# A decode step of attention beside a squared-ReLU MLP on one core: wq loaded ahead of the first K unit, output sums kept as two plain halves

## The chip, the core and the metric

The kernel runs on one core of a Trainium2 chip. The metric is device time in microseconds (us), as the median of three timed runs. "Faster" or "slower" is meant against that median. All instruction times come from one profiled execution of the kernel. In the names below, PE is TensorE's matmuls and PEld its weight loads, DVE is VectorE, ACT is ScalarE, POOL is GpSimd, and SP is SyncE, which here does nothing but issue transfers.

## What is computed

Two tokens (B = 2) of width D = 576 pass one layer norm, and the result feeds two branches whose outputs are added to the input.

```python
xn  = layernorm(x)                                  # 2 x 576
q   = xn @ wq                                       # 32 heads of 128
k,v = last 2048 positions of the caches, 16 heads, each shared by 2 query heads
A   = softmax(q k^T / sqrt(128)) v @ wo             # wo: 4096 x 576
h   = relu(xn @ w1 + b1); h = h * h                 # 4608 wide
B   = h @ w2 + b2                                   # w2: 4608 x 576
out = x + A + B                                     # 2 x 576, bf16
```

Everything is bf16 in memory. The windows of K and V are 16.8 MB each, and the four weight matrices add 20.1 MB, so that about 53.6 MB must be read for an output of 2.3 KB.

## The kernel before

**Units.** K and V are cut into eight units each, four heads of one batch row at a time. A unit is one transfer of 2 MB into one of six slots of a pool (`kvpool`, tag `kv`), 16 KB in each of 128 partitions. wq, w1 and wo share one slot of another pool (`wbig`), in that order. All these loads are issued by SP, in program order (lines 130 to 136, 415, 421, 426 to 433 and 435 to 441). A load into a slot that is in use waits in SP's queue until the slot's last reader is done, and every load behind it waits too.

**Start.** The order of the first loads is K unit 0 (line 130), wq (131), K1, V0, K2, V1, K3. Meanwhile the layer norm of x and a set of small masks and identities are made. PE then transposes K0 (`transposes(0, g)`, line 410: eight groups of four transposes into PSUM, copied out by ACT and DVE in turn), and after that `q_block` (line 411, defined at 226) computes q with 36 matmuls of 512 columns, copies the rows out (238), transposes them and spreads them into `qz` (254). Then come the scores and the softmax of unit 0 (lines 413 and 414).

**Steady part.** `step(u)` (line 387) transposes K unit u, with the product of probabilities and V of unit u-2 between the groups, then scores and softmax. `mlp_h` (356) computes h from w1 when w1 has landed (line 434), and puts it, transposed, into `hT_sb`. The result of attention stands, transposed, in `ws` (351).

**Output sums.** The sum `x + b2 + A + B` is accumulated in one PSUM tile `out_ps`. `out_acc` (216) takes one block of 128 rows of wo or w2, that is 576 columns, as four matmuls of 144 columns, one on each of the four strips of 32 columns of the array (`tile_position=(0, 32 * i)`). The two batch rows stand 16 partitions apart (`BS = 16`, `MB = 17`), so a weight operand has 17 columns, 15 of them zeros that two POOL memsets (310, 312) write at the start. The order on PE, which the program fixes (`keep_in_program_order`), is: 32 blocks of wo (line 446), 18 blocks of `w2a` (448), then 9 of `w2b` and 9 of `w2c` (451). `w2c` arrives by three transfers of 6, 2 and 1 blocks (`W2P`, line 76), the last loads of the kernel. So each of the blocks 9, 15 and 17 waits for a landing of its own.

**Store.** ACT issues one store of `w2b`'s first bytes to the output when w2b has landed (line 455), then casts `out_ps` to bf16 (456), 113 partitions by 144 columns, and stores the result over the first one (457), as a pattern of 4 quarters by 2 rows by 144 elements, that is, eight pieces of 288 bytes.

Of the kernel before, what the change touches and what calls it, by code (L numbers as in the profile page):

```python
# [8 lines left out]
F32 = mybir.dt.float32  # L9
BF16 = mybir.dt.bfloat16  # L10
ACT = mybir.ActivationFunctionType
ALU = mybir.AluOpType
AX = mybir.AxisListType
# [3 lines left out]
def kernel(  # L17
# [14 lines left out]
    nc = tc.nc  # L32
    P = 128
    B, Sq, D = A_x.shape
    _, Hkv, Sk, Dh = A_k_cache.shape
# [25 lines left out]
    NG4 = 4  # L61
# [10 lines left out]
    WR = Hq * Dh // P  # L72
    WC = Dh // WR
    FR = L1 // P
    assert HW == 32 * FR and QH * 2 == NC and NC * WC == 32
    W2P = [(9, 15), (15, 17), (17, 18)]
    R9 = 9
    BS = 16
    MB = BS * (B - 1) + 1
    RM = 32 * (NG4 - 1) + MB  # L80
    OQ = D // 4
    BIG = 1e30

    const = ctx.enter_context(tc.tile_pool(name="const", bufs=1))
# [4 lines left out]
    work = ctx.enter_context(tc.tile_pool(name="work", bufs=2))  # L89
    keep = ctx.enter_context(tc.tile_pool(name="keep", bufs=2))  # L90
    psum = ctx.enter_context(tc.tile_pool(name="psum", bufs=1, space=bass.MemoryType.PSUM))

    def matmul(*a, **k):
        tc.keep_in_program_order(nc.tensor.matmul(*a, **k))  # L94
# [15 lines left out]
    def load_k(u):  # L110
        issue_kv(k_tiles, A_k_cache, u, "k")
# [4 lines left out]
    def issue_flat(w, name):  # L116
        n = w.shape[0] * w.shape[1] // P
        tl = wbig.tile([P, NH * L1], BF16, tag="wbig", name=name)
        nc.sync.dma_start(out=tl[:, 0:n], in_=w.rearrange("r n -> (r n)").rearrange("(p l) -> p l", p=P))
        return tl  # L120

    const.tile([P, 144], F32, name="pad_0")
    xb_sb = const.tile([B + 1, D], BF16, name="xb_sb")
    x_sb = xb_sb[0:B, :]
    nc.scalar.dma_start(out=x_sb, in_=x2d)
# [1 line left out]
    nc.vector.memset(eps_t[:], 1e-5)  # L127
    warm = const.tile([B, 2], F32, name="warm")
    nc.scalar.activation(out=warm[:, 0:1], in_=eps_t[:], func=ACT.Sqrt)
    load_k(0)  # L130
    wq_sb = issue_flat(A_wq, "wq")
    load_k(1)
    load_v(0)
    load_k(2)
# [15 lines left out]
    nc.vector.tensor_scalar(out=ident[:], in0=col_f, scalar1=row_f[:, 0:1], scalar2=None, op0=ALU.is_equal)  # L150
    ident_f = const.tile([P, P], F32, name="ident_f")
    nc.vector.tensor_scalar(out=ident_f[:], in0=col_f[:], scalar1=row_f[:, 0:1], scalar2=None, op0=ALU.is_equal)
    sel_b = const.tile([B + 1, MB], BF16, name="sel_b")
    nc.vector.memset(sel_b[:], 0.0)
    nc.vector.memset(sel_b[:, 0:MB:BS], 1.0)
    nc.vector.tensor_copy(out=sel_b[0:B, 0:MB:BS], in_=ident[0:B, 0:B])

    half_d = D // 2
    stats = const.tile([B, 2, 6], F32, name="stats")
# [50 lines left out]

    w2c_sb = w2pool.tile([P, (FR - R9) * D], BF16, name="w2c")

    out_ps = psum.tile([RM, OQ], F32, tag="out", name="out_ps")
    nc.vector.memset(out_ps[:], 0.0)

    def out_acc(lhsT, rhs, o, start=False, stop=False):
        for i in range(4):
            matmul(out_ps[32 * i:32 * i + MB, :], lhsT=lhsT, rhs=rhs[:, o * D + i * OQ:o * D + (i + 1) * OQ],
                   start=start, stop=stop, skip_group_check=True, tile_position=(0, 32 * i))

    qz = const.tile([P, NQ, B, 2, 3 * QZ], BF16, name="qz")
    nc.gpsimd.memset(qz[:], 0.0)
    q_ps = psum.tile([P, QW], F32, tag="o", name="q_ps")
    nc.vector.memset(q_ps[:], 0.0)

    def q_block():
        for t in range(NH):
            for g in range(NG4):
                o = t * LQ + g * QW
                matmul(q_ps[32 * g:32 * g + 2 * B, :], lhsT=xnT[:, t].rearrange("p x b -> p (x b)"),  # L230
                       rhs=wq_sb[:, o:o + QW], start=(t == 0), stop=(t == NH - 1), skip_group_check=True,
                       tile_position=(0, 32 * g))
        row_t = const.tile([RB, 4 * HW], BF16, tag="row", name="qrow")
        qrow = row_t[:, 0:2 * QW]
        nh = QH // 2
        for k in range(2):
            cp = nc.scalar.copy if k else nc.vector.tensor_copy
            cp(out=qrow[:, k * QW:(k + 1) * QW].rearrange("p (i a d) -> p i a d", a=2, d=Dh),  # L238
               in_=q_ps[0:RB, k * QW // 2:(k + 1) * QW // 2].rearrange("p (i d) -> p i d", d=Dh).unsqueeze(2)
               .to_broadcast([RB, nh, 2, Dh]))  # L240
        qrow_f = qrow.bitcast(F32)
        qT_ps = psum.tile([P, QH * P], F32, tag="sc", bufs=2, name="qT_ps")
        for i in range(QH):
            transpose(out=qT_ps[:, i * P:i * P + RB], in_=qrow_f[:, i * Dh:(i + 1) * Dh],
                      identity=ident_f[0:RB, 0:RB])
        qT_v = qT_ps[:].bitcast(BF16).rearrange("p (i g e x b c) -> p b x g c e i", g=NG4 // 2, e=2, x=32 // B, b=B, c=2)
        hd = Dh // 2
        for j2 in range(2):
            cp = nc.scalar.copy if j2 else nc.vector.tensor_copy
            pp = slice(hd * j2, hd * (j2 + 1))  # L250
            o = QZ + NC * j2
            for b in range(B):
                for half in range(2):
                    cp(out=qz[pp, half * NQ // 2:(half + 1) * NQ // 2, b, :, o:o + NC].rearrange(  # L254
                        "p g c (e i) -> p g c e i", e=2), in_=qT_v[pp, b, half])
# [50 lines left out]
        pT_tiles[u] = pT  # L306
        o1_tiles[u] = o1

    ws = const.tile([P, WR, MB], BF16, name="ws")
    nc.gpsimd.memset(ws[:], 0.0)  # L310
    hT_sb = const.tile([P, 2, FR, MB], BF16, name="hT_sb")
    nc.gpsimd.memset(hT_sb[:], 0.0)

    def pv(u, part, parts):
        n = NJJ // parts
# [10 lines left out]
    def pv_end(u):  # L326
        tq, b = divmod(u, B)
        o_ps = o_tiles.pop(u)
        o1 = o1_tiles.pop(u)
        for k in range(NS):  # L330
            kw = dict(out=o1[:, 0:Dh], in0=o_ps[:, k * Dh:(k + 1) * Dh])
            if k == 0:
                nc.vector.tensor_scalar(scalar1=in_s[:, 0:1], scalar2=None, op0=ALU.mult, **kw)
            else:
                nc.vector.scalar_tensor_tensor(scalar=in_s[:, k:k + 1], in1=o1[:, 0:Dh], op0=ALU.mult, op1=ALU.add,  # L335
                                               **kw)

        def fin():
            op = psum.tile([P, Dh + 1], F32, tag="op", name=f"op_ps_{u}")
            pp = slice(32 * tq, 32 * (tq + 1))  # L340
            matmul(op[pp, :], lhsT=of_h[:], rhs=o1[:], start=True, stop=True, skip_group_check=True,
                   tile_position=(0, 32 * tq))
            linv = work.tile([P, 1], F32, tag="linv", name=f"linv_{u}")
            nc.vector.reciprocal(out=linv[pp, :], in_=op[pp, Dh:Dh + 1])
            om_t = work.tile([P, Dh], F32, tag="om", name=f"om_{u}")
            om = om_t[pp, :].rearrange("p (q r) -> p q r", r=WR)
            nc.vector.scalar_tensor_tensor(out=om, in0=op[pp, 0:Dh].rearrange("p (q r) -> p q r", r=WR),
                                           scalar=linv[pp, 0:1], op0=ALU.mult, op1=ALU.mult,
                                           in1=own_c[pp, :].unsqueeze(2).to_broadcast([32, WC, WR]))
            with nc.allow_low_precision(reason="sums of one term and zeros"):  # L350
                nc.vector.tensor_reduce(out=ws[pp, :, BS * b], in_=om.rearrange("p q r -> p r q"), axis=AX.X,  # L351
                                        op=ALU.add)

        return fin

    def mlp_h(w1_sb):
# [20 lines left out]
        for a in range(2):  # L377
            hp = psum.tile([P, nr, RB + 4], BF16, tag="sc", bufs=2, name=f"hp_{a}")
            for r in range(nr):
                transpose(out=hp[:, r, 0:RB], in_=hrow[:, a * nr + r:4 * HW:FR], identity=ident[0:RB, 0:RB])  # L380
            for g in range(NG4):
                pp = slice(32 * g, 32 * (g + 1))
                cp = nc.scalar.copy if g % 2 else nc.vector.tensor_copy
                cp(out=hT_sb[pp, :, a * nr:(a + 1) * nr, 0:MB:BS].rearrange("p x r b -> p r x b"),
                   in_=hp[pp, :, 32 * g:32 * g + 2 * B].rearrange("p r (x b) -> p r x b", b=B))

    def step(u):
# [17 lines left out]
    def pv_all(u):  # L405
        pv(u, 0, 1)
        pv_end(u)()

    for g in range(NG):
        transposes(0, g)  # L410
    q_block()
    for t in range(NT):
        scores(0, t)
    softmax(0)
    load_v(2)
    b1_rows = B_b1.rearrange("(x n) -> x n", n=HW)
    for i0, i1 in ((0, 2), (2, 4), (4, 6), (6, 8)):
        nc.scalar.dma_start(out=b1_sb[i0:i1, :], in_=b1_rows[i0:i1, :])
    nc.scalar.dma_start(out=xb_sb[B:B + 1, :], in_=B_b2.rearrange("(o n) -> o n", o=1))
    step(1)  # L420
# [21 lines left out]
    step(NU - 1)  # L442
    pv_all(NU - 2)
    pv_all(NU - 1)
    for r in range(WR):
        out_acc(ws[:, r, :], wo_sb, r)
    for r in range(FR):
        out_acc(hT_sb[:, 0, r, :], w2a_sb, r)
    for r in range(FR):
        w, o = (w2b_sb, r) if r < R9 else (w2c_sb, r - R9)  # L450
        out_acc(hT_sb[:, 1, r, :], w, o, stop=(r == FR - 1))

    fin_sb = work.tile([RM, OQ], BF16, tag="fin", name="fin_sb")
    out_v = out2d.rearrange("b (q n) -> q b n", q=4)
    nc.scalar.dma_start(out=out_v, in_=w2b_sb[0:RM:BS, 0:OQ])
    nc.scalar.copy(out=fin_sb[:], in_=out_ps[:])  # L456
    nc.scalar.dma_start(out=out_v, in_=fin_sb[0:RM:BS, :])


# [28 lines left out]
```

## Time and profile before

| | us |
|---|---|
| timed runs | 134.02, 134.00, 133.95 (median 134.0) |
| profiled execution, first to last instruction (span) | 132.1 |
| median less span: what lies around the span | 1.9 |
| PE, DVE, ACT busy | 84.6, 63.2, 46.7 |
| HBM read over the span | 53.62 MB, 406 GB/s |
| last matmuls (w2c) begin, in the span | 127.90 |
| cast of the output, begin | 129.29 |
| store of the output issued | 129.60 |

The profiled execution has no time of its own beside its span, so 1.9 us is the distance from that span to the median of the three runs. The profile has a page of totals, a list of what ended each wait, a chain of work that ended last, a timeline, and tables by window, that is, busy times in stretches of time that one chooses. In tables by window, the columns are the stretch, its length, the busy time of each engine with its instructions in brackets, the clock that TensorE was granted (1.00 is full speed), the mean busy share of the 16 DMA engines, and GB/s. All times count from the first instruction.

### The profile page before, as it was taken

To read this page: it belongs to the slowest core of one execution; us is meant where nothing else is said; L and a number is where in the kernel's file an instruction comes from. 1 tells how busy PE (TensorE), PEld (TensorE's weight loads), DVE (VectorE), ACT (ScalarE), POOL (GpSimd) and SP (SyncE) were. 2 spreads that over 40 slices of the span, in tenths; PEclk is the share of its full clock that TensorE was granted. 3 is DMA by queue.
4 is the path that set the end of the run, shared out by engine and by line. 5 is a ranking of instruction groups with operands and counts; after the bars stand their busy time and mean duration, and the time that the engine had idled before them with its cause. 6 is when DMAs were issued, how large, how long until landed. Compare 5 with 4: busy or idle time off the path is not lost.

```text
span 132.1 us, 2285 instructions
## 1 busy us (share of the span) xinstructions
PE 84.6 (64%) x949; PEld 52.6 (40%) x949; DVE 63.2 (48%) x176; ACT 46.7 (35%) x67; POOL 4.9 (4%) x15
## 2 busy tenths in 40 slices
PE   0089319599589687697599787104819972739471
PEld 0069202286345353363455443002417640229360
DVE  7764400344557677396547687410075667550000
ACT  5725400339566085283256094200106632000000
POOL 5000000010010100100100100100000001000000
PEclk9999955959999999999779999855695999555955
DMA  4999899999999999999999999999999999899960
GB/s 160 397 437 526 369 388 442 422 432 432 429 432 422 442 417 427 437 432 437 432 427 414 437 488 402 445 424 405 427 427 442 468 435 458 376 408 418 418 255 1
DMA packets 3511, 53.76 MB, mean 407 GB/s; under 512 B 419, under 2 KB 558, under 8 KB 814
## 3 DMA queue, kind: packets, MB, share of 16 engines
q1 hardware_dynamic: 3456, 53.61, 95.2%
q8 instruction: 7, 0.11, 0.3%
q10 hardware_dynamic: 46, 0.02, 0.1%
q14 instruction: 2, 0.02, 0.0%
HBM read 53.62 MB, written 0.00 MB: 406 GB/s over the span
## 4 chain that ended last, share of the span: by engine, by line
DMA 78%; PE 15%; ACT 2%; SPq 1%; DVE 1%; issue 1%; ACTq 0%; DVEq 0%
DMA w<-in_B_w_dram 25%; DMA w2c<-in_B_w_dram 24%; DMA k<-in_A_k_cache_dram 16%; DMA wq<-in_A_wq_dram 13%; PE kT_ps L97 5%; PE h_ps L94 3%; PE q_ps L94 3%; PE sc_ps L94 2%; PE out_ps L94 1%; PE o_ps L94 1%; ACT kT L270 1%; DVE qrow L238 1%; SPq L106 0%; ACT qrow L238 0%; DVE qz L254 0%
## 5 line engine op out<-in xcount | busy, mean ns | idle before, releaser
L97 PE MATMUL kT_ps<-ident_f,k 128*128 128x128 f32 x256 | 41.4, 312 | 5.7 <-DMA k<-in_A_k_cache_dram 3.9
L97 PEld LDWEIGHTS kT_ps<-ident_f,k 128*128 128x128 f32 x256 | 32.9, 161 | 18.8 <-issue 9.9
L270 ACT COPY kT<-kT_ps 128x1024 bf16<-128x1024 bf16 x32 | 31.9, 1012 | 17.8 <-PE kT_ps L97 17.8
L272 DVE COPY kT<-kT_ps 128x1024 bf16<-128x1024 bf16 x32 | 21.8, 682 | 6.4 <-PE kT_ps L97 6.1
L94 PE MATMUL sc_ps<-kT,qz 128*32 128x512 bf16 x128 | 9.9, 388 | 6.7 <-DVE kT L272 4.7
L302 ACT ACTIVATE p<-sc_ps,bias 128x512 bf16<-128x512 f32 x8 | 5.5, 688 | 21.4 <-DVE gown L298 18.2
L94 PE MATMUL o_ps<-v,pT 128*32 128x512 bf16 x128 | 11.2, 429 | 0.0
L94 PEld LDWEIGHTS <-xnT 128*4 128x4 bf16 x108 | 3.5, 121 | 16.8 <-issue 15.2
L94 PE MATMUL h_ps<-w,xnT 128*4 128x288 bf16 x72 | 4.3, 429 | 8.0 <-DMA w<-in_B_w_dram 8.0
L305 DVE STREAM_TRANSPOSE pT<-p 128x512 bf16<-128x512 bf16 x8 | 5.7, 710 | 6.2 <-ACT p L302 6.2
L335 DVE SCALAR_TENSOR_TENSOR o<-o_ps,in_s,o 128x128 f32<-128x128 f32 x24 | 8.3, 345 | 0.4
L291 DVE TENSOR_REDUCE m<-sc_ps 128x1 f32<-128x512 f32 x8 | 5.5, 692 | 4.8 <-PE sc_ps L94 4.8
L375 DVE TENSOR_TENSOR hrow<-t 100x1152 bf16<-100x1152 f32 x2 | 2.6, 1355 | 9.6 <-ACT t L373 9.6
L94 PE MATMUL q_ps<-wq,xnT 128*4 128x512 bf16 x36 | 4.0, 627 | 4.9 <-DMA wq<-in_A_wq_dram 4.9
L295 POOL PARTITION_ALL_REDUCE gmax<-m x8 | 2.9, 367 | 104.9 <-DVE m L293 104.9
L94 PE MATMUL op_ps<-o,of_h 128*32 128x129 f32 x16 | 3.7, 316 | 4.6 <-DVE o L335 4.6
L456 ACT CAST fin_sb<-out_ps 113x144 bf16<-113x144 f32 x1 | 0.3, 280 | 17.9 <-PE out_ps L94 17.9
L94 PEld LDWEIGHTS <-qz 128*32 128x32 bf16 x128 | 2.1, 94 | 10.4 <-DVE kT L272 7.2
L97 PE MATMUL pro_ps<-ident,xn_sb 2*128 2x2 bf16 x5 | 0.9, 182 | 6.8 <-DVE xn_sb L171 6.5
L94 PEld LDWEIGHTS <-hT_sb 128*17 128x17 bf16 x144 | 3.4, 108 | 3.6 <-issue 3.5
L94 PE MATMUL out_ps<-wo,ws 128*17 128x144 bf16 x128 | 4.0, 325 | 1.2 <-DVE ws L351 1.2
L238 DVE CAST qrow<-q_ps 100x512 bf16<-100x512 f32 x1 | 0.7, 692 | 8.2 <-PE q_ps L94 8.2
(71 smaller groups left out, 57.4 us busy)
## 6 DMA issues: line engine op xcount, KB each, us to landing
k<-in_A_k_cache_dram SPq DMA_DIRECT2D x8, 2048.0 KB, 21.0
v<-in_A_v_cache_dram SPq DMA_DIRECT2D x8, 2048.0 KB, 21.5
w<-in_B_w_dram SPq DMA_DIRECT2D x1, 5184.0 KB
wq<-in_A_wq_dram SPq DMA_DIRECT2D x1, 4608.0 KB, 17.8
wo<-in_A_wo_dram SPq DMA_DIRECT2D x1, 4608.0 KB
w2a<-in_B_w_dram SPq DMA_DIRECT2D x1, 2592.0 KB, 26.9
w2b<-in_B_w_dram SPq DMA_DIRECT2D x1, 1296.0 KB
w2c<-in_B_w_dram SPq DMA_DIRECT2D x1, 864.0 KB
```

Source lines behind the costliest of these rows:

```text
L94: tc.keep_in_program_order(nc.tensor.matmul(*a, **k))
L97: tc.keep_in_program_order(nc.tensor.transpose(*a, **k))
L238: cp(out=qrow[:, k * QW:(k + 1) * QW].rearrange("p (i a d) -> p i a d", a=2, d=Dh), in_=q_ps[0:RB, k * QW // 2:(k + 1) * QW // 2].rearrang ...
L270: nc.scalar.copy(out=kT, in_=kT_ps[:])
L272: nc.vector.tensor_copy(out=kT, in_=kT_ps[:])
L291: nc.vector.tensor_reduce(out=m1[:], in_=sc_ps[:], axis=AX.X, op=ALU.max)
L295: nc.gpsimd.partition_all_reduce(gmax[:], m2[:], channels=P, reduce_op=ReduceOp.max)
L302: nc.scalar.activation(out=p_sb[:], in_=sc_ps[:], func=ACT.Exp, bias=bias[:, 0:1], scale=scale, accum_out=o1[:, Dh:Dh + 1])
L305: nc.vector.transpose(out=pT[:].rearrange("p j r -> p (j r)"), in_=p_sb[:])
L335: nc.vector.scalar_tensor_tensor(scalar=in_s[:, k:k + 1], in1=o1[:, 0:Dh], op0=ALU.mult, op1=ALU.add, **kw)
L375: nc.vector.tensor_tensor(out=h4[:, :, k * HB:(k + 1) * HB], in0=t4, in1=t4, op=ALU.mult)
L456: nc.scalar.copy(out=fin_sb[:], in_=out_ps[:])
```

## The change

**Start.** wq is issued ahead of K0. `q_block` is split into `q_rows` (the 36 matmuls) and `q_place` (copies, transposes and spreading), and both now stand ahead of the transposes of K0. b1 is loaded by three transfers and not four (3, 3 and 2 rows).

**Output sums.** The batch rows stand on neighbouring partitions, so that the weight operand has 2 columns, and the two zeroing POOL memsets go. `out_acc` takes a block as two matmuls of 288 columns on strips 0 and 1. For wo and w2a, odd blocks go to a second PSUM tile, `pre_ps`, on strips 2 and 3. After w2a, ACT copies `pre_ps` to SBUF, and two float32 matmuls with the identity add it into `out_ps`. The blocks of w2b and w2c use strips 0 and 1 alone. Between w2b and w2c stand three matmuls of 512 columns whose results nobody reads (`spin_ps`).

**Store.** The cast covers 34 partitions by 288 columns. ACT stores the left half, SP the right half, two rows of 576 bytes each.

**Slots.** The pad at the head of the constant pool grows from 144 to 152 elements. In the built programs the six K/V slots start at 31232 + n x 16384 before and at 29184 + n x 16384 after; the wbig slot at 129536 and 127488. All are multiples of 512.

```diff
-    BS = 16
-    MB = BS * (B - 1) + 1
-    RM = 32 * (NG4 - 1) + MB
-    OQ = D // 4
+    HD = D // 2
+    RO = 32 + B
+    RP = 96 + B
...
-    const.tile([P, 144], F32, name="pad_0")
+    const.tile([P, 152], F32, name="pad_0")
...
+    wq_sb = issue_flat(A_wq, "wq")
     load_k(0)
-    wq_sb = issue_flat(A_wq, "wq")
     load_k(1)
...
-    out_ps = psum.tile([RM, OQ], F32, tag="out", name="out_ps")
+    out_ps = psum.tile([RO, HD], F32, tag="out", name="out_ps")
...
-    def out_acc(lhsT, rhs, o, start=False, stop=False):
-        for i in range(4):
-            matmul(out_ps[32 * i:32 * i + MB, :], lhsT=lhsT, rhs=rhs[:, o * D + i * OQ:o * D + (i + 1) * OQ],
-                   start=start, stop=stop, skip_group_check=True, tile_position=(0, 32 * i))
+    def out_acc(lhsT, rhs, o, start=False, stop=False, acc=out_ps, base=0):
+        for i in range(2):
+            p = base + 32 * i
+            matmul(acc[p:p + B, :], lhsT=lhsT, rhs=rhs[:, o * D + i * HD:o * D + (i + 1) * HD], start=start,
+                   stop=stop, skip_group_check=True, tile_position=(0, p))
...
-    ws = const.tile([P, WR, MB], BF16, name="ws")
-    nc.gpsimd.memset(ws[:], 0.0)
-    hT_sb = const.tile([P, 2, FR, MB], BF16, name="hT_sb")
-    nc.gpsimd.memset(hT_sb[:], 0.0)
+    ws = const.tile([P, WR, B], BF16, name="ws")
+    hT_sb = const.tile([P, 2, FR, B], BF16, name="hT_sb")
...
+    q_rows()
+    q_place()
     for g in range(NG):
         transposes(0, g)
-    q_block()
...
-    for i0, i1 in ((0, 2), (2, 4), (4, 6), (6, 8)):
+    for i0, i1 in ((0, 3), (3, 6), (6, 8)):
...
+    pre_ps = psum.tile([RP, HD], F32, tag="sc", bufs=2, name="pre_ps")
+    nc.vector.memset(pre_ps[:], 0.0)
+    pre_sb = work.tile([P, HD], F32, tag="t1", name="pre_sb")
+    nc.gpsimd.memset(pre_sb[:], 0.0)
+    spin_ps = psum.tile([P, 512], F32, tag="sc", bufs=2, name="spin_ps")
+    def out_alt(lhsT, rhs, r, start=False, stop=False):
+        if r % 2:
+            out_acc(lhsT, rhs, r, start=start, stop=stop, acc=pre_ps, base=64)
+        else:
+            out_acc(lhsT, rhs, r)
     for r in range(WR):
-        out_acc(ws[:, r, :], wo_sb, r)
+        out_alt(ws[:, r, :], wo_sb, r, start=(r == 1))
     for r in range(FR):
-        out_acc(hT_sb[:, 0, r, :], w2a_sb, r)
+        out_alt(hT_sb[:, 0, r, :], w2a_sb, r, stop=(r == FR - 1))
+    nc.scalar.copy(out=pre_sb[64:RP, :], in_=pre_ps[64:RP, :])
+    for i in range(2):
+        p = 64 + 32 * i
+        matmul(out_ps[32 * i:32 * i + B, :], lhsT=ident_f[:, p:p + B], rhs=pre_sb[:], start=False, stop=False,
+               skip_group_check=True, tile_position=(0, 32 * i))
     for r in range(FR):
         w, o = (w2b_sb, r) if r < R9 else (w2c_sb, r - R9)
         out_acc(hT_sb[:, 1, r, :], w, o, stop=(r == FR - 1))
+        if r == R9 - 1:
+            for _ in range(3):
+                matmul(spin_ps[0:B, :], lhsT=ws[:, 0, :], rhs=wo_sb[:, 0:512], start=True, stop=True,
+                       skip_group_check=True)
...
-    fin_sb = work.tile([RM, OQ], BF16, tag="fin", name="fin_sb")
-    out_v = out2d.rearrange("b (q n) -> q b n", q=4)
-    nc.scalar.dma_start(out=out_v, in_=w2b_sb[0:RM:BS, 0:OQ])
+    fin_sb = work.tile([RO, HD], BF16, tag="fin", name="fin_sb")
+    nc.scalar.dma_start(out=out2d[:, 0:HD], in_=w2b_sb[0:B, 0:HD])
     nc.scalar.copy(out=fin_sb[:], in_=out_ps[:])
-    nc.scalar.dma_start(out=out_v, in_=fin_sb[0:RM:BS, :])
+    nc.scalar.dma_start(out=out2d[:, 0:HD], in_=fin_sb[0:B, :])
+    nc.sync.dma_start(out=out2d[:, HD:D], in_=fin_sb[32:RO, :])
```

More of the change, by code (lines that the diff above doesn't have):

```diff
@@ L152 @@
     nc.vector.tensor_scalar(out=ident_f[:], in0=col_f[:], scalar1=row_f[:, 0:1], scalar2=None, op0=ALU.is_equal)
[L153 to L156, printed above, removed]
+    sel_b = const.tile([B + 1, B], BF16, name="sel_b")
+    nc.vector.memset(sel_b[:], 1.0)
+    nc.vector.tensor_copy(out=sel_b[0:B, :], in_=ident[0:B, 0:B])
     half_d = D // 2
@@ L224, with q_rows @@
     nc.vector.memset(q_ps[:], 0.0)
-    def q_block():
+    def q_rows():
         for t in range(NH):
@@ L232, in q_block, with q_place @@
                        tile_position=(0, 32 * g))
+    def q_place():
         row_t = const.tile([RB, 4 * HW], BF16, tag="row", name="qrow")
@@ L350, in fin @@
             with nc.allow_low_precision(reason="sums of one term and zeros"):
-                nc.vector.tensor_reduce(out=ws[pp, :, BS * b], in_=om.rearrange("p q r -> p r q"), axis=AX.X,
+                nc.vector.tensor_reduce(out=ws[pp, :, b], in_=om.rearrange("p q r -> p r q"), axis=AX.X,
                                         op=ALU.add)
@@ L383, in mlp_h @@
                 cp = nc.scalar.copy if g % 2 else nc.vector.tensor_copy
-                cp(out=hT_sb[pp, :, a * nr:(a + 1) * nr, 0:MB:BS].rearrange("p x r b -> p r x b"),
+                cp(out=hT_sb[pp, :, a * nr:(a + 1) * nr, :].rearrange("p x r b -> p r x b"),
                    in_=hp[pp, :, 32 * g:32 * g + 2 * B].rearrange("p r (x b) -> p r x b", b=B))
```

## The prediction

> **What bounds the kernel now.** I read the totals of DMA first, then the chain that ended last, then the end of the timeline.
>
> ```profile
> DMA  4999899999999999999999999999999999899960
> q1 hardware_dynamic: 3456, 53.61, 95.2%
> q8 instruction: 7, 0.11, 0.3%
> k<-in_A_k_cache_dram SPq DMA_DIRECT2D x8, 2048.0 KB, 21.0
> ```
>
> The 16 DMA engines are busy from the second slice almost to the last. By window, they show a share of 1.00 and 426 GB/s from 2.60 to 127.90. Moreover the loads are queued deep: a K unit of 2.1 MB needs 2.1 / 0.426 = 4.9 us of the stream, but lands 21.0 us after its issue (median). Some 16 us of other loads lie ahead of it. So a load that is issued up to about 16 us later costs nothing, and what the compute engines do in the middle does not set the end. The chain says the same:
>
> ```profile
> 33.63 20.86 DMA k<-in_A_k_cache_dram
> ...
> 96.74 31.12 DMA w2c<-in_B_w_dram
> ...
> 127.90 1.36 PE out_ps L94 x36
> ...
> 129.29 0.28 ACT fin_sb L456
> ```
>
> Its last transfer is w2c; then 36 matmuls, the cast, the store. These 36 look like a chain of matmuls, but three landings hide in them. The timeline from 129.05 on shows the last four alone:
>
> ```profile
> 128.95 0.30 PE L94 MATMUL out_ps<-w2c,hT_sb 128*17 128x144 bf16 x4
> ```
>
> The block before began at 128.69 (a window that opens at 128.9 shows that as its first matmul), and blocks follow each other every 0.12 us when nothing is missing (block 16 begins 0.11 after block 15, at 128.59). Block 17 thus waited 0.14 us or more for its own piece of w2c, and the path is: last piece usable at 128.95, four matmuls of 0.30, cast, store. PE's speed on w2c costs nothing as long as it is idle when the last piece lands.
>
> **The stream: -0.05, bounds -0.6 and +0.2.** The same bytes go by the same queue. The first issue stays at 0.72 and only changes from K0 to wq. Slots are on multiples of 512 before and after, so this part changes nothing that a transfer could feel. b1 goes by one small transfer fewer; b1, x and b2 are a few KB. PE has fewer instructions (1152 rows against 1421 in listings of the two programs that merge equal neighbours, so roughly). If q8 fetches code for PE, its seven packets (0.3% of 16 x 132.1 us, about 0.9 us of one engine each) become five or six. Spread over 16 engines one is worth 0.06 us; on the engine that finishes last, with the others close behind, perhaps 0.6. I take -0.05.
>
> **The start: 0.** wq and K0 land as a pair at the time the pair landed before (19.19, the landing of wq in the chain). wq alone: 4.7 MB / 0.426 = 11.1 us after 2.1, plus the 1.0 by which K0's landing (8.05) was later than its bytes (2.1 + 4.9), so about 14.2. q_rows (36 matmuls, 4.04) ends near 18.3; qrow on DVE and ACT (0.70 + 0.59), the transposes (0.41) and qz (0.49, beside ACT's 0.44) end near 20.9. K0's 32 transposes, which took from 8.08 to 14.83 with their copies, now stand behind these on PE, ACT and DVE and end near 26.5 to 27; the scores end near 28, against 27.20. So PE is 0.5 to 0.8 us late. Behind K0's transposes in the queues stands only the load of V2, which needs K0's slot: on SP it moves from 19.27 to about 27, and the loads behind it stay where they are (K4 was issued at 33.63). Seven loads, 17.3 MB, are issued before; by 27 the stream has moved 10.6 MB, so 15 us of it are left. PE's own lateness ends at 53.41, where it waited 1.22 us for K4. If that cover were gone, the start would cost its 0.8 us.
>
> **wo and w2a: 0.** One block costs what it did: four strips at 144 columns, or two blocks on four strips at 288. wo then ends near 122.3, ahead of w2a's landing (122.73).
>
> ```profile
> L94 PE MATMUL h_ps<-w,xnT x72: 287/444/448, 91.1 to 95.1; 128*4 128x288 bf16 x72
> ```
>
> This row has exactly the new shape, 288 columns on four strips: 287 ns at full clock, 444 at half (minimum and median). 72 of them in 4.30 us make 0.239 us per round of four at half clock; at full clock, twice w2a's 62 ns per 144-column block, so 0.122. w2a: 9 rounds, 1.1 us, to 123.9. Then new: ACT's copy of pre_ps (0.41, the row of L373 with 288 columns, and 0.2 to hand over), then float32 matmuls. The nearest, op_ps with 129 columns, takes 0.41 for its two passes at full clock; 288 columns and two strips make about 0.75. That ends at 125.3, and w2b's landing is at 125.82: hidden by 0.5 us. Before, PE sat idle here without a wait from 123.8 to 125.3; should that stall stay, w2b would start up to 1 us late, and 0.4 us of it would show. The memset of pre_ps on DVE (98 x 288, near 0.3 by q_ps's 0.49 for 512 columns) stands in the last step's queue, ahead of unit 5's reciprocal; if all of it reached the last `ws`, and so the start of wo (118.36), the 0.35 us between wo's end and w2a's landing would take it in.
>
> **w2b, the spin, w2c: 0 at full clock.** On two strips, w2b takes 9 x 0.122 = 1.1 us to 126.95, three 512-column matmuls 3 x 0.215 = 0.65 (half of q_ps's pace of 0.43) to 127.6, and w2c can start at its landing, 127.90. Blocks 9 to 14 end at 128.63, 15 and 16 at 128.88, and block 17 starts at 128.95 as now, taking 0.287 against 0.30: -0.01. At half clock all of this is late (rival 1). So the clock decides:
>
> ```profile
> 23.33:26.74 3.41, 1.86 (x21) 1.00 1.01 432
> 26.74:30.15 3.41, 3.41 (x22) 0.50 1.02 432
> 50.63:54.04 3.41, 2.00 (x18) 1.00 0.99 423
> 54.05:57.46 3.41, 2.83 (x29) 1.00 0.99 423
> ...
> 118.90:122.31 3.41, 3.41 (x116) 0.50 0.98 420
> 122.31:125.72 3.41, 1.54 (x76) 1.00 0.98 409
> 125.73:129.14 3.41, 2.54 (x74) 0.50 0.55 216
> ```
>
> These are PE's rows by window, cut where the granted clock changes: length, busy time and matmuls, clock, DMA. The clock holds for 3.41 us and follows the window before. At full clock 2.00 us of work kept it, 1.86 and 1.54 lost it. In the last such window the changed kernel has w2a (1.25 with its drain) and the float32 matmuls (0.75): 2.00, at the edge. Cut anywhere else, most windows hold more, since wo, or w2b and the spin, come in. So full clock is likely, not safe.
>
> The Trainium skill ("TensorE: Matmul & The Clock Gate", Part 1) puts the loss of the clock after an idle window of about 3.4 us. By that rule alone PE would have been at full clock on w2c before already, and the spin would buy nothing; the row at 125.73 with 0.50 after 1.54 us of work says otherwise, and the row decides. By the rule the sum would be the same, with rival 1 gone.
>
> **Cast and store: -0.05.** The cast goes from 144 columns (0.28) to 288: 0.41 by L373, so +0.12. The store's issue was 0.54 on ACT; plain two-dimensional issues took 0.25 to 0.31 (b1), 0.42 (w2a) and 0.58 (w1): I take 0.42, -0.12, bounds -0.25 and +0.1. SP's half runs beside it. Two pieces of 576 bytes and not eight of 288: no row shows what a piece costs at the end; between 0 and the 2.3 us that SP waited for this store, nearest to 0 as both stores move 2.3 KB: -0.05, bounds -0.3 and +0.2.
>
> The skill ("DMA: Bandwidth & Descriptors", Issuing engines are not separate DMA queues) says that a second issuing engine saves only issue time; by it the split of the store is worth nothing beyond the 0.12, and the sum would be 0.05 higher. No run here shows it yet.
>
> **Sum.** -0.05 - 0.01 + 0.12 - 0.12 - 0.05 = -0.11. The span goes from 132.1 to 132.0 and, with the 1.9 around it, 134.0 to **133.9**. A measurement of this kernel can tell about 0.2% (0.27 us) from no change.
>
> **Rivals.** (1) *Half clock on w2b*, slower: in the window before 125.8 PE works under about 1.9 us of 3.41. Then w2b takes 9 x 0.239 = 2.15, to 127.97, the spin 3 x 0.43 = 1.28, to 129.25, w2c 1.3 at full or 2.35 at half clock. PE ends at 130.5 to 131.6 against 129.25: 135.2 to 136.3. For it: 2.00 is at the edge. Against it: other cuts of the window. A partly slow end lies between, from 134.3 on. (2) *The stream ends sooner*, faster: fewer packets for code, or a calmer order of the engines, move the last landing by 0.3 to 0.6, and everything behind it: 133.3 to 133.6. For it: from 127.1 to 127.9 the DMA share is already 0.48, so a few late engines set the end. Against it: the remaining packets can make the same engines late. (3) *The store is cheaper* than I take, by its whole bound: 0.25 + 0.3 - 0.12 = -0.43, 133.6; nothing in the profile shows it.
>
> **Numbers.** The forecast (within 0.2%) 0.54; rivals 2 and 3 together 0.24; rival 1 with its partial forms 0.22. The range takes in 2, 3 and rival 1 to its lower price: 133.3 to 135.2. The likeliest case alone is 133.73 to 134.27.
>
> **What would show it.** Right: the last w2c matmuls begin at 128.9 to 129.0 at a granted clock of 1.00, wait for a landing, and the cast follows 0.3 us later and takes 0.4; K4 is issued near 34 with no hole in the DMA row. Wrong: 0.50 in PE's window on w2b, w2c matmuls without a wait, or a last landing that has moved by more than 0.2 us.

## The result, and the profile after

| | before | after |
|---|---|---|
| median of 21 runs each, us | 134.01 | 133.79 |
| lowest to highest, us | 133.87 to 134.25 | 133.58 to 134.21 |
| span of the profiled execution, us | 132.1 | 132.0 |

The ratio is 0.9982, with a 95% interval of 0.9976 to 0.9988: 0.24 us less. It lies in the prediction's likeliest case, within 0.2%, 0.1 us below its 133.9. The small sum hides larger terms, though, and they are not all those of the forecast. First the totals of DMA of the changed kernel:

```profile
DMA  6998999999999999999999999998999999999960
q1 hardware_dynamic: 3460, 53.61, 95.6%
q8 instruction: 6, 0.10, 0.3%
k<-in_A_k_cache_dram SPq DMA_DIRECT2D x8, 2048.0 KB, 20.7
```

The stream is as full as it was, loads lie as long in the queues (20.7 us and not 21.0), and q8 has six packets instead of seven. The chain that ended last has the same end:

```profile
33.44 20.99 DMA k<-in_A_k_cache_dram
...
97.11 30.82 DMA w2c<-in_B_w_dram
127.93 0.04 issue
127.97 1.42 PE out_ps L93 x18
129.39 0.02 issue
129.42 0.39 ACT fin_sb L476
```

The cast takes 0.39 (0.28 before), and begins 0.13 later. That the last block waits for its landing is seen in the timeline from 129.1 to 129.3, with the 0.17 us in which the weight loads had nothing to do:

```profile
128.84 0.54 PE L93 MATMUL out_ps<-w2c,hT_sb 128*2 128x288 bf16 x4
129.09 0.08 PEld L93 LDWEIGHTS <-hT_sb 128*2 128x2 bf16 x1 [0.17 <-issue]
```

The first of these lines holds blocks 16 and 17; block 17 begins at 129.09, where it began at 128.95 before. So up to the cast's end the changed kernel is later in its profile, by 0.13 and 0.11, and still its span is 0.1 shorter. What is left is the store. Its issue stands in the timeline, first of the kernel before, then of the changed one:

```profile
129.60 0.54 ACTq L457 DMA_DIRECT2D out_dram<-fin_sb  x1
```

```profile
129.83 0.33 SPq L478 DMA_DIRECT2D out_dram<-fin_sb  x1
129.84 0.26 ACTq L477 DMA_DIRECT2D out_dram<-fin_sb  x1
```

The DMA view from 129.5 to 131.5, in 40 slices of 0.05 us, shows when its bytes move. First the kernel before, then the changed one:

```profile
GB/s 0 0 0 0 0 0 0 0 0 0 0 0 0 0 0 0 0 0 0 0 0 0 0 0 0 6 35 6 0 0 0 0 0 0 0 0 0 0 0 0
```

```profile
GB/s 0 0 0 0 0 0 0 0 0 0 0 0 0 0 0 0 0 0 0 0 0 12 35 0 0 0 0 0 0 0 0 0 0 0 0 0 0 0 0 0
```

Before, they move in slices 25 to 27 (130.75 to 130.90); after, in 21 and 22 (130.55 to 130.65). By the trace's records of single packets, the first one starts 1.19 us after the start of the issue in before, and 0.74 (ACT) or 0.79 (SP) in the changed kernel. From the start of the cast to the end of the last packet it is 1.60 before and 1.26 after: 0.33 less, although the cast is 0.11 longer. I call this stretch the *tail*. By the trace's records of semaphores, the landing (both stores landed, which SP waits for) follows the last packet by 0.33 before and by 0.44 after (SP's half; ACT's took 0.32), so that from the start of the cast to the landing it is 1.93 and 1.71: 0.22 less. From there to the end of the span both take 0.83. So the span's 0.1 is 0.13 more up to the cast and 0.22 less behind it.

### The profile page after: what moved, and what is told of

Read it like the earlier page. It is cut to its first block, busy times and chain, and to the rows that moved or that the text cites. A ratio compares the mean times of both kernels' runs of the same rounds, so it can differ in the third digit from the quotient of the medians.

```text
span 132.0 us, 2025 instructions
## 1 busy us (share of the span) xinstructions
PE 83.1 (63%) x818; PEld 46.1 (35%) x818; DVE 62.9 (48%) x176; ACT 46.6 (35%) x68; POOL 4.2 (3%) x14
## 4 chain that ended last, share of the span: by engine, by line
DMA 75%; PE 14%; ACT 5%; SPq 1%; issue 1%; DVE 1%; ACTq 0%; DVEq 0%
DMA w<-in_B_w_dram 25%; DMA w2c<-in_B_w_dram 23%; DMA k<-in_A_k_cache_dram 16%; DMA wq<-in_A_wq_dram 11%; PE kT_ps L96 4%; PE h_ps L93 3%; ACT kT L271 3%; PE q_ps L93 3%; PE sc_ps L93 2%; PE out_ps L93 1%; ACT L303 1%; PE o_ps L93 1%; DVE qrow L239 1%; ACT qrow L239 0%; SPq L105 0%
## 5 line engine op out<-in xcount | busy, mean ns | idle before, releaser
L96 PE MATMUL kT_ps<-ident_f,k 128*128 128x128 f32 x256 | 38.0, 290 | 7.1 <-DMA k<-in_A_k_cache_dram 4.5
L96 PEld LDWEIGHTS kT_ps<-ident_f,k 128*128 128x128 f32 x256 | 28.6, 146 | 21.7 <-issue 10.0
L93 PE MATMUL o_ps<-v,pT 128*32 128x512 bf16 x128 | 11.7, 449 | 0.0
L239 ACT CAST qrow<-q_ps 100x512 bf16<-100x512 f32 x1 | 0.6, 585 | 13.6 <-DVE qrow L239 13.6
L332 DVE TENSOR_SCALAR o<-o_ps,in_s 128x128 f32<-128x128 f32 x8 | 2.7, 343 | 4.7 <-PE o_ps L93 4.7
## 6 DMA issues: line engine op xcount, KB each, us to landing
k<-in_A_k_cache_dram SPq DMA_DIRECT2D x8, 2048.0 KB, 20.7
```

Source lines behind the costliest of these rows:

```text
L96: tc.keep_in_program_order(nc.tensor.transpose(*a, **k))
```

## Experiments

All were compared with the kernel before, run beside them on the same chip. "Tail" and "landing", the time from the start of the cast to the landing, are read from the one profile of each run (before: 1.60 and 1.93); "time" is the ratio's distance from 1, in us. The theories: the **store** makes the gain, less the wider cast; the **start** makes it; the spin, and with it the **clock**, does.

| run | median, us | ratio (95%) | time | tail, us | landing, us |
|---|---|---|---|---|---|
| changed kernel | 133.79 | 0.9982 (0.9976 to 0.9988) | -0.24 | 1.26 | 1.71 |
| head_only | 134.04 | 0.9998 (0.9989 to 1.0007) | -0.03 | 1.60 | 1.94 |
| tail_only | 133.91 | 0.9989 (0.9980 to 0.9997) | -0.15 | 1.26 | 1.71 |
| quarters_two_queues | 134.45 | 1.0030 (1.0019 to 1.0041) | +0.40 | 1.90 | 2.23 |
| no_spin | 133.72 | 0.9977 (0.9967 to 0.9987) | -0.31 | 1.27 | 1.71 |
| halves_one_queue | 133.91 | 0.9988 (0.9979 to 0.9997) | -0.16 | 1.52 | 1.84 |
| halves_one_store | 134.25 | 1.0017 (1.0008 to 1.0026) | +0.23 | 1.67 | 2.00 |
| two_casts | 133.86 | 0.9987 (0.9978 to 0.9996) | -0.17 | 1.33 | 1.70 |
| rows_two_queues | 134.49 | 1.0026 (1.0017 to 1.0035) | +0.35 | 1.92 | 2.24 |
| rows_neighbours | 134.33 | 1.0016 (1.0003 to 1.0028) | +0.21 | 1.92 | 2.25 |
| slots_off | 134.89 | 1.0063 (1.0050 to 1.0075) | +0.84 | 1.27 | 1.71 |
| slots_64 | 134.56 | 1.0030 (1.0017 to 1.0043) | +0.40 | 1.26 | 1.70 |
| no_pre | 133.95 | 1.0000 (0.9976 to 1.0023) | 0.00 | 1.26 | 1.71 |

### The start alone

```diff
+    wq_sb = issue_flat(A_wq, "wq")
     load_k(0)
-    wq_sb = issue_flat(A_wq, "wq")
...
+    q_block()
     for g in range(NG):
         transposes(0, g)
-    q_block()
...
-    for i0, i1 in ((0, 2), (2, 4), (4, 6), (6, 8)):
+    for i0, i1 in ((0, 3), (3, 6), (6, 8)):
```

> The kernel before with the changed start alone: wq ahead of K0, q ahead of K0's transposes, b1 by three transfers; output sums and store as before. Store theory (the 0.24 us come from the store, 0.33 less from the cast's end to the landing, less 0.11 for the wider cast): 134.0, within 0.1 of before, last piece of w2c usable at 128.9 to 129.1. Start theory (the start orders the stream better): 133.8, the last piece usable 0.2 earlier than in a run of before. In both, K4 is issued near 33.5 and the scores of unit 0 end near 27.

Measured 134.04, no change, with the last four w2c matmuls 0.18 later in its profile. The start theory falls.

### All but the start

The changed kernel with the diff above taken back.

> The changed kernel with the start of before: K0 ahead of wq, K0's transposes ahead of q, b1 by four transfers. Store theory: 133.8, as the changed kernel; the cast takes 0.39, and SP sees the store land 1.3 us after the cast's end. Start theory: 134.0.

Measured 133.91, with the tail of the changed kernel. Against the changed kernel's 133.79 the intervals overlap: a share of the start of about 0.1 us can't be excluded here, but head_only shows none (-0.03, with an interval from -0.15 to +0.09).

### Two queues, the pieces of before

```diff
-    nc.scalar.dma_start(out=out_v, in_=fin_sb[0:RM:BS, :])
+    nc.scalar.dma_start(out=out_v[0:2], in_=fin_sb[0:32 + MB:BS, :])
+    nc.sync.dma_start(out=out_v[2:4], in_=fin_sb[64:RM:BS, :])
```

> The kernel before with one edit: of the four quarters of the output, ACT stores two and SP two, still in pieces of 288 bytes; the cast stays at 113 x 144 and 0.28 us. If it is the shorter issues on two queues that save, it gets the store's gain without the wider cast: 133.7, SP seeing the landing about 1.35 us after the cast's end and not 1.67. If it is the size and number of the pieces, 134.0. Start theory: 134.0.

Measured 134.45: neither of the two, but slower than before. From its timeline:

```profile
129.36 0.28 ACT L456 CAST fin_sb<-out_ps 113x144 bf16<-113x144 f32 x1 [17.54 <-PE out_ps L94]
129.66 0.66 SPq L458 DMA_DIRECT2D out_dram<-fin_sb  x1
129.67 0.54 ACTq L457 DMA_DIRECT2D out_dram<-fin_sb  x1
```

Half the pieces left ACT's issue at 0.54. SP takes 0.66 over a store of this kind, and its first packet comes 1.55 us after the start of the issue, against 1.19 on ACT. The DMA view from 129.5 to 131.5 has ACT's half in slice 27 (130.85) and SP's in slice 34 (131.20):

```profile
GB/s 0 0 0 0 0 0 0 0 0 0 0 0 0 0 0 0 0 0 0 0 0 0 0 0 0 0 0 23 0 0 0 0 0 0 23 0 0 0 0 0
```

So a second queue is no gain as such.

### One queue, the pieces of after

```diff
-    nc.sync.dma_start(out=out2d[:, HD:D], in_=fin_sb[32:RO, :])
+    nc.scalar.dma_start(out=out2d[:, HD:D], in_=fin_sb[32:RO, :])
```

> The changed kernel, but ACT issues both halves of the output, one after the other, where SP issued the right one. If the second queue saves issue time, the second half is issued 0.26 us later (one issue of ACT in the changed profile) and the time is 134.0 to 134.1. If it is the plain shape and the larger pieces alone, 133.8.

```profile
129.38 0.39 ACT L476 CAST fin_sb<-out_ps 34x288 bf16<-34x288 f32 x1 [4.75 <-PE out_ps L93]
129.80 0.25 ACTq L477 DMA_DIRECT2D out_dram<-fin_sb  x1
130.10 0.27 ACTq L478 DMA_DIRECT2D out_dram<-fin_sb  x1
```

The second issue comes 0.29 later (one issue and the step between). The tail is 0.26 longer than in the changed kernel, and the landing 0.13. The time, 133.91, is 0.1 above the changed kernel's, as the landing has it, though their intervals overlap; it is 0.16 below before. The Trainium skill's "DMA: Bandwidth & Descriptors" (Issuing engines are not separate DMA queues) grants a second engine just the time of the issue. That agrees with the bytes, 0.26 earlier for issues of 0.25, of which the landing keeps half. In the case of the quarters the second engine's issue costs more than it saves: 0.3 us of tail.

### One store, pieces of 576 bytes

The changed kernel with `BS = 16` again (17 columns in a weight operand, and the zeroing memsets), a pad of 16 elements, and the edit below. Packets of the K/V units take the 611 ns (median) of the changed kernel, so the place of the slots is not in play.

```diff
-    nc.scalar.dma_start(out=out2d[:, 0:HD], in_=fin_sb[0:B, :])
-    nc.sync.dma_start(out=out2d[:, HD:D], in_=fin_sb[32:RO, :])
+    nc.scalar.dma_start(out=out2d.rearrange("b (h n) -> h b n", h=2), in_=fin_sb[0:RO:BS, :])
```

> The changed kernel with its batch rows 16 partitions apart (17 columns in a weight operand), so that both halves go by one store of ACT: two halves by two rows of 288 elements, four pieces of 576 bytes, from every 16th partition. If the issue of a pattern over such rows is what was dear (0.54 in before), it stays at 0.45 to 0.55, and the time is 134.0 to 134.1. If the number and size of the pieces make the gain, 133.8.

```profile
129.75 0.53 ACTq L483 DMA_DIRECT2D out_dram<-fin_sb  x1
```

Measured 134.25, its issue 0.53 and its first packet 1.17 after the start of the issue: nearly the numbers of before, with half as many pieces, twice as large. The size of the pieces gives nothing, nor does going from eight of them to four.

### The cast on two engines

```diff
-    nc.scalar.copy(out=fin_sb[:], in_=out_ps[:])
+    nc.scalar.copy(out=fin_sb[0:B, :], in_=out_ps[0:B, :])
+    nc.vector.tensor_copy(out=fin_sb[32:RO, :], in_=out_ps[32:RO, :])
```

> The changed kernel with the cast split: ACT casts the left half, which it stores itself, DVE the right half, which SP stores. An ACT or DVE operation takes as long as its 288 columns, not its partitions, so ACT's stays at 0.39; DVE's is 0.3 to 0.45 by its copies from PSUM. Store theory: within 0.1 of the changed kernel, 133.75. If the sharing of a whole tile by two waiting stores costs, it shows here as an earlier issue of one half.

Measured 133.86. ACT's cast of 2 partitions takes the 0.39 of 34; DVE's takes 0.45, and SP's issue comes 0.1 after ACT's. The landing is that of the changed kernel. Nothing is won.

### No spin

`for _ in range(3)` becomes `range(0)`.

> The changed kernel without the three matmuls whose results nobody reads. My prediction's picture of the clock, 2.00 us of work in a window keeps full speed and 1.54 to 1.86 lose it: the window before the last holds less work without the 0.81 us of the spin, but in the changed profile it is w2a and the blocks of w2b that stand in it; I expect w2c at full clock still and 133.8. Clock theory: the spin is what holds the clock; w2c runs at half clock, 18 matmuls of w2c's first blocks at 0.239 a round end near 129.5 to 130.1 and not before the last landing, the time is 134.3 to 135.

Measured 133.72, at least as good. These are PE's rows by window of its profile, cut where the clock's windows begin (stretch, length, PE's busy time and matmuls, clock, DMA share, GB/s); the second has wo's last blocks, w2a and the start of the float32 matmuls, the third their end, w2b and the first blocks of w2c:

```profile
117.93:121.34 3.41, 3.16 (x56) 0.50 0.99 426
121.34:124.75 3.41, 1.93 (x54) 1.00 0.97 407
124.75:128.16 3.41, 2.03 (x28) 1.00 0.79 320
128.17:131.58 3.41, 1.13 (x18) 1.00 0.02 7
```

1.93 and 2.03 us of work keep full speed without the spin. The clock theory falls for the spin; in the changed kernel it is surplus. Of all versions this one has the lowest median, but its interval holds the changed kernel's ratio.

### Without the second sum tile

Every block of wo and w2a goes by `out_acc` on strips 0 and 1; `pre_ps`, its copy and the two float32 matmuls are left out.

> The changed kernel with every block of wo and w2a on strips 0 and 1, without the second sum tile, its copy and its two float32 matmuls. The blocks of w2b take 0.122 us at full clock on two strips and 0.239 at half. 50 blocks of wo and w2a then take 6.1 to 12 us from 118.9; at half clock for one window of 3.41 and full speed after, wo ends near 124.5, w2a near 126.7, w2b and the spin near 128.5, w2c near 130.6, 1.2 us later than in the changed kernel: 134.9 to 135.3. If PE had cover enough, as my prediction's price of 0 for this part would have it for any layout: 133.8.

Measured 133.95, but from 133.54 to 135.31 over twelve runs, five of them at 134.3 or more. The profiled execution (133.66) was a good one. Its timeline:

```profile
118.09 5.97 PE L93 MATMUL out_ps<-wo,ws 128*2 128x288 bf16 x64 [1.06 <-DVE ws L350]
123.90 2.37 PE L93 MATMUL out_ps<-w2a,hT_sb 128*2 128x288 bf16 x36
126.10 1.27 PE L93 MATMUL out_ps<-w2b,hT_sb 128*2 128x288 bf16 x18
127.21 0.81 PE L93 MATMUL spin_ps<-wo,ws 128*2 128x512 bf16 x3
127.93 1.36 PE L93 MATMUL out_ps<-w2c,hT_sb 128*2 128x288 bf16 x18
```

PE runs from 118.09 to the first landing of w2c without a pause, and is just in time. My expectation of 134.9 to 135.3 was reached by one run only, at 135.31. That the others were late on PE, for a clock that rose later, is argued: no profile caught one. The second tile buys a time that stays below 134.25 rather than a lower median.

### Slots off the multiple of 512

```diff
-    const.tile([P, 152], F32, name="pad_0")
+    const.tile([P, 144], F32, name="pad_0")
```

> The changed kernel with the pad at 144 elements, as before: all slots of K, V, w and w2 move by 32 bytes, from multiples of 512 to 32 bytes short of one. Store theory and the prediction's view, that the slots move nothing that a transfer feels: 133.8, DMA at 407 GB/s. If the place of a slot matters to a transfer: slower, each per cent of the stream being 1.3 us.

Measured 134.89, 1.1 us above the changed kernel. The tail is the same; the stream ends later, and evenly so. DMA by window of this run, then of the changed kernel (columns: stretch, length, clock, DMA share, GB/s):

```profile
0.00:33.00 33.00, 1.00 0.95 399
33.00:66.00 33.00, 1.00 1.01 427
66.00:100.00 34.00, 0.71 1.00 427
```

```profile
0.00:33.00 33.00, 1.00 0.96 399
33.00:66.00 33.00, 0.95 1.01 430
66.00:100.00 34.00, 0.75 1.01 431
```

430 and 431 GB/s have become 427, at a share that is full in both: packets take longer. The median of those of 16384 bytes goes from 611 to 614 ns, of 10368 from 389 to 398, and of the code packets on q8 from 929 to 1081. Summed over all packets and spread over 16 engines that is 0.63 us, of the 0.88 by which block 17 begins later; where the rest comes from stays open. The pad moves the small tiles behind it too; that the loads make the loss is read from their packets, and from PE, which waits for w2c.

### Slots 64 bytes off

The same pad at 136 elements.

> The changed kernel with all slots 64 bytes short of a multiple of 512, where the run with the pad of before had them 32 short and took 134.89, with the stream's end 0.77 later in its profile and most packets longer by 0.1 to 2.3 per cent. If 64 bytes are grain enough for the writes: 133.8. If it needs 512: 134.9. Between them, if the cost goes with the part of pieces that a boundary cuts.

Measured 134.56, between the two: 64 bytes are not grain enough, and the cost is a little less than at 32. The Trainium skill ("DMA: Bandwidth & Descriptors", How a descriptor splits into AXI transactions) says that a descriptor not starting on a multiple of 256 bytes pays for bytes it doesn't use. By its counting, an estimate, 16384 bytes starting 32 short of such a multiple take 519 beats and not 512, 64 short 518: 1.4 and 1.2%. The page speaks of bytes that are fetched, while here the off-grain side is the one written, in SBUF. By the medians the runs stand 0.8 and 0.6% above the changed kernel (0.8 and 0.5% by the ratios): the direction and the order agree, and the size measured is about half. Which grain is enough, 128, 256 or 512, was not tried.

### Rows on two queues, plain

The kernel before, stored by rows, so that the pattern is plain but from four partitions 32 apart:

```diff
+    out_v = out2d.rearrange("b (q n) -> b q n", q=4)
-    nc.scalar.dma_start(out=out_v, in_=fin_sb[0:RM:BS, :])
+    nc.scalar.dma_start(out=out_v[0], in_=fin_sb[0:97:32, :])
+    nc.sync.dma_start(out=out_v[1], in_=fin_sb[BS:RM:32, :])
```

> The kernel before with one edit in its store: ACT stores batch row 0 and SP batch row 1, each from four partitions 32 apart in order into 1152 bytes that are whole in DRAM, so as a plain two-dimensional pattern, in four pieces of 288 bytes; the cast stays 0.28. Theory that the shape of the pattern decides (a store's first packet moves 0.74 us after the start of its issue in the changed kernel, 1.19 in before and also in the four quarters and the four halves): issues of 0.26 to 0.33, first packet after 0.75, the last about 1.2 us after PE's end, 0.4 less than before: 133.65. Theory that the number of pieces decides (two pieces in the changed kernel, four or eight in the slow ones): issues of 0.54 and 0.66 as with the quarters, 134.1 to 134.45.

```profile
129.59 0.28 ACT L456 CAST fin_sb<-out_ps 113x144 bf16<-113x144 f32 x1 [17.07 <-PE out_ps L94]
129.90 0.66 SPq L458 DMA_DIRECT2D out_dram<-fin_sb  x1
129.90 0.52 ACTq L457 DMA_DIRECT2D out_dram<-fin_sb  x1
```

Measured 134.49, with issues of 0.52 and 0.66 and first packets 1.17 and 1.54 after their start. A plain pattern alone is not what makes the store cheap.

### Rows, neighbouring batch rows, four strips throughout

The store of the last run with the changed start, `BS = 1`, no zeroing memsets, a pad of 152; no second tile and no spin. It was meant as a version that beats both.

> The store of the run with one row per queue, in a kernel with the changed start, neighbouring batch rows, no zeroing memsets, four strips of 144 columns throughout, no second sum tile, no spin, slots on multiples of 512. By the store theory the time is that of the run with one row per queue, within 0.1, since neither the start nor the width of the weight operand is on the path: 133.65 if the shape decides. If the neighbouring rows or the spin bring something of their own, it stands apart from that run by 0.15 or more.

Measured 134.33, 0.16 below the last run with intervals that touch, and slower than before. The tail of 1.92 is the same, so weights of 2 columns, the memsets and the start change nothing in the tail.

## What made the time

The way from the cast to the landing explains the sign of every run in which it changed, and most of the size in nearly all (the runs with other slots, and no_pre, whose time scatters with PE, apart). Where it is 0.22 or 0.23 shorter than before, the time is 0.15 to 0.31 less; where it is 0.30 to 0.32 longer, 0.21 to 0.40 more. In halves_one_queue the two are -0.09 and -0.16, in halves_one_store +0.07 and +0.23. What is left over, 0.16 us at most, is no more than the stream's end scatters from profile to profile: with slots on multiples of 512, block 17 begins between 128.94 (tail_only) and 129.25 (rows_two_queues), and neither the old nor the new start owns the early or the late ones.

The tail is set by the kind of store:

| store | issue on ACT, SP | first packet after the start of the issue |
|---|---|---|
| two rows of 576 bytes, neighbouring partitions | 0.25 to 0.27, 0.32 to 0.33 | 0.73 to 0.75, 0.76 to 0.80 |
| 4 x 2 or 2 x 2 x 288 bytes, partitions 16 and 32 apart | 0.54, 0.66 | 1.19, 1.55 |
| 2 x 2 x 576 bytes, partitions 16 and 32 apart | 0.53 | 1.17 |
| 4 x 288 bytes, plain, partitions 32 apart | 0.52, 0.65 to 0.66 | 1.17, 1.53 to 1.54 |

The size of the pieces does not set it (third row), nor does a plain pattern by itself (fourth). Every dear store reads partitions that are not neighbours, and every cheap one neighbours. But every cheap store also has two pieces, and every dear one four or eight. Against the number as the cause of a long issue speaks a load: SP issues the last one of w2c, 128 pieces of 1152 bytes to 128 neighbouring partitions, in 0.33 us, as its store of two. For the time to the first packet no run decides between neighbours, the number of pieces, and a plain pattern together with large pieces. Two rows of 576 bytes from partitions 16 apart, and four rows from neighbours, would settle it; neither was tried. Nor is the kind of transfer all that counts: x's load, two neighbouring rows on ACT, took 0.54 us over its issue at 0.73, beside SP's first issue.

## The prediction, step by step

- **Stream, -0.05:** not resolved. One packet of code fewer came true; the last piece came 0.14 later in the profile, which is within the scatter of its start, and the time leaves 0.02 for it (-0.24 against the -0.22 up to the landing). Rival 2, a stream that ends sooner, did not come.
- **Slots, nothing to feel:** right between these two kernels, and only since both are on multiples of 512. The pad of before, kept, would have cost 1.1 us.
- **Start, 0:** right (head_only), with one term mis-sized. I had PE 0.5 to 0.8 late and the scores ending near 28; they end at 27.05, against 27.20. I priced K0's transposes and copies by their stretch in before, 6.75 us from the first to the last copy's end, where a transpose took 421 ns (median of 32), and 273 only from 13.2 on, 5 us after PE had begun. Behind q, with PE at work since 15.00, they took 273 from the first on, and ran from 20.41 to 25.65: 5.2 us, against 6.3 in before. K4 was issued at 33.44, as foreseen.
- **wo and w2a, 0:** right, with the cover overstated. w2a ran mostly at half clock, the float32 matmuls ended near 125.9 and not 125.3, level with w2b's landing. The 0.5 us were gone, and nothing showed, as w2b and the spin still ended 0.1 before the landing of w2c.
- **Full clock on w2b and w2c:** right. PE's rows of the changed kernel, by the clock's windows:

```profile
117.35:120.76 3.41, 2.35 (x34) 0.50 1.00 432
120.77:124.17 3.40, 3.40 (x60) 0.50 0.96 406
124.18:127.58 3.40, 2.84 (x45) 1.00 0.89 360
127.60:131.00 3.40, 1.64 (x20) 1.00 0.12 44
```

  Rival 1 had no window to start from. The edge that I read off before's rows, full clock kept at 2.00 and lost at 1.86, does not hold, though. In the changed kernel itself 1.87 kept it (first two rows) and 2.02 lost it (last two):

```profile
69.57:72.98 3.41, 1.87 (x17) 1.00 1.00 423
72.98:76.39 3.41, 2.11 (x20) 1.00 0.99 423
79.80:83.21 3.41, 2.02 (x18) 1.00 1.07 462
83.21:86.62 3.41, 0.00 (x0) 0.50 0.93 394
```

  The busy time of a window alone does not decide. That 1.54 lost it in before stands; what does decide near 2 us was not found.
- **Cast, +0.12:** 0.39 against 0.28, +0.11.
- **Store issue, -0.12:** mis-sized; -0.29 on ACT, beyond its bound of -0.25, and -0.21 on SP. I took w2a's 0.42 as the nearest plain issue, where the b1 issues of 0.25 to 0.31, two neighbouring rows each, were the same kind of transfer; they stood in the text as the bound.
- **Pieces, -0.05:** the step failed. The size of the pieces gives nothing, nor does having four for eight. What came instead are two stretches that the sum did not have. From the end of the issue to the first packet it is 0.65 before, and 0.49 on ACT and 0.46 on SP after; from the last packet to the landing 0.33 before and 0.44 after. For SP's half, which lands last, that makes -0.40 up to its first packet, -0.04 over its packets and +0.11 up to the landing: -0.33, where the two terms had -0.17. With the cast it is -0.22, between the sum's -0.05 and rival 3's -0.43. The forecast held since this error of 0.16 is smaller than the 0.27 that it allowed, and not because the store was priced rightly.

## What to carry to other kernels

Once a kernel is bound by a stream to its last byte, what remains to be won lies behind the last landing: read the final store's issue, the time to its first packet and the time from its last packet to the landing, and price a new store by an issue with the same partitions and pattern, not by one of similar size. Splitting a store over two engines saves at most one issue, half of it by the landing here, and loses when the second engine's issue of that kind is slower. And when an edit shrinks a constant pool, look at where the large load slots then start.

## What the runs showed of the chip that I had not expected

- SP is slower than ACT on the same dear store: issue 0.66 against 0.54, first packet after 1.55 against 1.19. On the cheap store the first packets differ by 0.05 only (0.79 against 0.74).
- The first packet lags the end of the issue by 0.43 to 0.49 us for the cheap stores, 0.65 for dear ones on ACT and 0.88 to 0.89 on SP: a dear issue costs again after it has ended.
- Slots 32 or 64 bytes off a multiple of 512 cost 0.8 and 0.5 to 0.6% of the whole time, and the code packets, on a queue of their own, took 16% longer in the first of these runs (1081 against 929 ns).
- A cast of 288 columns takes 0.39 us on ACT for 2, 34 or 49 partitions alike, and 0.45 on DVE for 2.
- PE kept full clock through a window of 3.41 us with 1.87 us of matmuls and lost it after one with 2.02, in the same execution.
